# Which of the block-diagonal q rows go by VectorE copy and which by transfer: two and two in each half, against one and three, then three and one

## The chip, the cores and the metric

The kernel runs on one core of one Trainium2 chip. The metric is the device time of one execution in microseconds (us), less is better. Before the change it was 1295.35 us (median of 5 runs, 1295.15 to 1295.88). Timed runs were of the fast state (within 1.5% of the fastest of the same kernel); the four single looks near the end are of unknown state, as a single run of one core always is.

## The reference, cut to what matters

Two layers, each an attention block and a token-mixing MLP, on 2048 tokens of width 1024. The change is in the attention block only. It has 32 heads of width 32, and each token sees eight tokens, its own and those 2, 4, ... 14 places back:

```python
off = jnp.arange(8) * 2
idx = pos[:, None] - off[None, :]
...
logits = jnp.einsum("bhsd,bhswd->bhsw", q, kg) * scale
attn = _softmax(jnp.where(mask, logits, -1e9), axis=-1)
o = jnp.einsum("bhsw,bhswd->bhsd", attn, vg)
```

## The kernel before

Even and odd tokens never meet, so a *unit* is one parity (1024 tokens) of one group of four heads (128 of the 1024 columns): 16 units a layer. Work on a unit is done in two *visits* of 512 tokens each; they are numbered 0 to 63 over both layers, and even ones begin a unit. In each visit TensorE does the scores of this unit, the values of the visit before, and two of the four query/key chunks of the **next** unit. Queries of both halves (n = 0, 1) are made in the first visit, keys in the second.

The scores of four heads are had from one matmul because q is laid out block-diagonally: `qB[u % 2]` has 128 partitions by four head blocks, and in head block h only partitions 32h to 32h+31 are not zero. So each half's q, which arrives as one 128x512 tile `qs`, has to be put into four places of 32 partitions each.

```python
    def qk_chunk(u, wts, part, n):
        ...                                     # eight matmuls into ps   (L352)
        ls = slice(n * 512, (n + 1) * 512)
        if part:
            nc.scalar.copy(out=kT[u % 2][:, ls], in_=ps[:])               # L356
        else:
            qs = gop.tile([P, 512], BF16, name="qs", tag="go")
            nc.scalar.copy(out=qs[:], in_=ps[:])                          # L359
            for h in range(HG):
                hp = slice(h * DH, (h + 1) * DH)
                if h < HG // 2 or u == 0:                                 # the changed line
                    nc.vector.tensor_copy(out=qB[u % 2][hp, h, ls], in_=qs[hp, :])            # L363
                else:
                    chain_("SP", lambda: nc.sync.dma_start(out=qB[u % 2][hp, h, ls], in_=qs[hp, :]))  # L365
        return mm

    def scores(u, b):
        ...
        for i in range(HB):                     # 4
            lo = (b * HB + i) * P
            for r in range(P // KG):            # 4: sixteen matmuls a visit
                ...
                mm = nc.tensor.matmul(dst, lhsT=k[:, lo + r * KG:lo + (r + 1) * KG],
                                      rhs=q[:, :, lo + r * KG:lo + r * KG + GW], start=True, stop=True)   # L383
        ...                                     # exponential on ScalarE (L386); mask on VectorE (L398)
```

GW is 40, 32 tokens and 8 more. So in the first visit of a unit only the sixteenth score matmul reads into the second half of q, by eight columns. The PSUM accumulator of the values is a pool of one; `norm` (L437, VectorE) has to read it before the next visit's values matmuls (L414, L418) may write it.

The softmax here doesn't subtract the row's maximum and nothing guards it: scores larger than these inputs give would overflow.

## Time and profile before

| | before |
|---|---|
| time, median of 5 | 1295.35 us |
| TensorE busy | 1276.5 of 1293.7 us |
| attention, first to last start of a query/key matmul | 139.96 + 139.34 = 279.30 us |
| one unit, median (scores of a visit to those of the second after it) | 8.86 us |
| copies into qB | 136, 282 ns each (median) |
| transfers into qB | 120, 1.8 us (median) from issue to landing, when all of the data has arrived |

The profile page of the kernel before: busy time by engine, then instruction packets in the queues, the chain of waits, and two groups of instructions (count, then busy us and mean ns of one, then idle time of the engine before them and what ended most of it).

```profile
PE 1276.5 (99%) x8286; PEld 593.7 (46%) x8442; DVE 417.3 (32%) x852; ACT 373.2 (29%) x628; POOL 2.4 (0%) x15
...
q8 instruction: 66, 1.08, 0.3%
...
PE 98%; issue 1%; DVE 0%; DMA 0%; ACT 0%; SPq 0%
...
L352 PE MATMUL m<-hT,wqk 128*128 128x512 bf16 x963 | 223.3, 379 | 6.2 <-issue 4.6
L363 DVE COPY qB<-qs 32x512 bf16<-32x512 bf16 x136 | 38.1, 280 | 90.5 <-ACT qs L359 89.2
```

TensorE is the bound; VectorE is busy a third of the time. A matmul's 379 ns is not its cost: in a stream one starts every 0.216 us. (The Trainium skill, "Perfetto Trace Analysis", warns at its head that matmul busy time is a bad metric because matmuls are pipelined; this trace agrees, 379 against 216 ns.) Hence lengths of stretches are used below, not busy time.

The view of stretches for the two attention stretches (columns: start:end, length, then busy time of PE, PEld, DVE, ACT, POOL with counts, clock, DMA share, GB/s):

```profile
66.43:206.39 139.96, 136.37 (x1735) 67.08 (x1763) 95.85 (x217) 91.01 (x152) 0.00 (x0) 1.00 0.19 55
706.54:845.88 139.34, 136.13 (x1733) 67.08 (x1763) 95.85 (x217) 90.91 (x152) 0.00 (x0) 1.00 0.20 56
```

Where TensorE waited for transfers shows in its list of waits over the attention of the first layer (total us, times, longest):

```profile
PE m L352 <- issue: 2.4, 15, 0.2
PE s L383 <- DMA qB<-qs: 0.4, 1, 0.4
```

And in the timeline of that unit (start, length, engine and line; in brackets the idle time before and what ended it):

```profile
156.39 2.87 SPq L365 DMA_DIRECT2D qB<-qs  x4
...
156.95 0.57 DVE L363 COPY qB<-qs 32x512 bf16<-32x512 bf16 x2
...
158.13 0.58 DVE L363 COPY qB<-qs 32x512 bf16<-32x512 bf16 x2 [0.60 <-ACT qs L359]
158.82 2.02 DVE L398 TENSOR_TENSOR Pm<-pc,band 32x640 bf16<-32x640 bf16 x4
160.88 0.69 DVE L437 TENSOR_TENSOR oT<-acc,rd 128x512 bf16<-128x512 f32 x1
...
161.81 0.46 PE L383 MATMUL s<-qB,kT 128*32 128x160 bf16 x15
...
162.63 0.23 PE L383 MATMUL s<-qB,kT 128*32 128x160 bf16 x1 [0.36 <-DMA qB<-qs]
```

Fifteen score matmuls start in time, and the sixteenth 0.81 us after the first, where 0.23 us is usual. It waited for the last of the four transfers. Normally that transfer, issued 3.14 us ahead of the scores, lands 1.3 us ahead of them; here it was issued at 158.67 and landed at 162.49, 3.8 us later. Three more units have this in a smaller size, too small for the list of waits: visits 18, 44 and 46, by 0.29, 0.07 and 0.20 us. With the 0.58 us of this one (visit 20), TensorE lost 1.14 us.

The DMA view of 160.3 to 161.5 us of the same trace (packets, MB, share):

```profile
DMA packets 3, 0.02 MB, mean 15 GB/s; under 512 B 0, under 2 KB 2, under 8 KB 2
...
q8 instruction: 1, 0.02, 4.6%
q1 hardware_dynamic: 2, 0.00, 1.3%
```

Only one packet is under way at first: a 16,384-byte packet of the instruction queue (a block of instructions being fetched) starts at 160.44 and takes 0.88 us, and only as it ends do two small packets of the transfer start. The packet records behind this view say more. The transfer is 32 packets of 1,024 bytes; 30 of them had started, and these two are the rest. A packet's record here does not name its DMA engine; that the two sat behind the fetch on one engine is read from this order.

### The profile page before, as it was taken

What the parts mean: (1) busy time and instruction counts of PE and PEld (TensorE: products, weight loads), DVE (VectorE), ACT (ScalarE), POOL (GpSimd) and SP (SyncE); (2) the same over time, 40 slices, a digit from 0 to 9 for tenths busy, and PEclk for the clock granted to TensorE, in tenths of its full rate; (3) what the DMA queues carried; (4) which work ended last, traced back from release to release, by engine and by line L of the source; (5) the groups of instructions that cost most, each with busy time, mean ns of one, the idle gap of its engine ahead of it and who ended that gap; (6) DMA issues with size and microseconds to landing.
All of it is one profiled execution on the core that took longest, in us unless ns stands there. A gap on an engine that the chain in (4) does not pass through costs nothing.

```text
span 1293.7 us, 19400 instructions
## 1 busy us (share of the span) xinstructions
PE 1276.5 (99%) x8286; PEld 593.7 (46%) x8442; DVE 417.3 (32%) x852; ACT 373.2 (29%) x628; POOL 2.4 (0%) x15
## 2 busy tenths in 40 slices
PE   9999999999999999999999999999999999999999
PEld 4444444444444444444444444444444444444444
DVE  7457767830000022322300667778100000111111
ACT  5456665541111100000023666644311111000000
POOL 0000000000000000000000000000000000000000
PEclk9999999999999999999999999999999999999999
DMA  7411123643222135456510111246422222334331
GB/s 236 82 44 48 51 80 122 204 138 90 65 78 80 57 101 148 124 155 147 130 33 1 46 51 49 80 151 209 125 66 86 78 59 78 105 106 135 118 92 33
DMA packets 201862, 125.54 MB, mean 97 GB/s; under 512 B 39984, under 2 KB 183600, under 8 KB 201776
## 3 DMA queue, kind: packets, MB, share of 16 engines
q1 hardware_dynamic: 201776, 124.30, 33.9%
q8 instruction: 66, 1.08, 0.3%
q14 instruction: 20, 0.16, 0.0%
HBM read 96.48 MB, written 16.78 MB: 88 GB/s over the span
## 4 chain that ended last, share of the span: by engine, by line
PE 98%; issue 1%; DVE 0%; DMA 0%; ACT 0%; SPq 0%
PE m L352 17%; PE s L594 15%; PE s L547 15%; PE m L467 8%; PE acc L547 7%; PE m L547 7%; PE acc L594 7%; PE m L594 7%; PE m L337 4%; PE m L255 4%; PE s L383 2%; PE acc L418 1%; PE acc L422 1%; PE m L268 0%; DMA qB<-qs 0%
## 5 line engine op out<-in xcount | busy, mean ns | idle before, releaser
L594 PEld LDWEIGHTS <-w 128*128 128x128 bf16 x1820 | 177.0, 98 | 210.2
L547 PEld LDWEIGHTS <-w 128*128 128x128 bf16 x1792 | 175.4, 98 | 211.4
L352 PE MATMUL m<-hT,wqk 128*128 128x512 bf16 x963 | 223.3, 379 | 6.2 <-issue 4.6
L547 PE MATMUL s<-h,w 128*128 128x512 bf16 x878 | 201.2, 379 | 0.8
L594 PE MATMUL s<-g,w 128*128 128x512 bf16 (+1 forms) x912 | 201.0, 374 | 0.7
L596 DVE SCALAR_TENSOR_TENSOR xo<-s,b_sb,xs 128x512 bf16<-128x512 f32 (+1 forms) x33 | 24.4, 739 | 532.9 <-PE s L594 527.6
L352 PEld LDWEIGHTS <-wqk 128*128 128x128 bf16 x1024 | 95.3, 98 | 117.9 <-issue 10.7
L398 DVE TENSOR_TENSOR Pm<-pc,band 32x640 bf16<-32x640 bf16 x256 | 123.5, 483 | 66.0 <-ACT pc L386 56.6
L467 PE MATMUL m<-wo,oT 128*128 128x512 bf16 x500 | 110.6, 379 | 0.8 <-issue 0.3
L547 PE MATMUL acc<-h,w 128*128 128x512 bf16 x440 | 103.1, 379 | 0.5
L594 PE MATMUL acc<-g,w 128*128 128x512 bf16 x436 | 99.7, 379 | 0.5
L547 PE MATMUL m<-h,w 128*128 128x512 bf16 x438 | 98.5, 379 | 0.5
L594 PE MATMUL m<-g,w 128*128 128x512 bf16 (+1 forms) x436 | 96.9, 376 | 0.6
L174 ACT ACTIVATE ln<-mv,eps 128x1 f32<-128x1 f32 x64 | 18.9, 295 | 221.1 <-DVE mv L182 184.9
L467 PEld LDWEIGHTS <-oT 128*128 128x128 bf16 x512 | 49.6, 98 | 60.3 <-issue 1.3
L554 ACT ACTIVATE g<-s,b_sb 128x1024 bf16<-128x1024 f32 x28 | 31.2, 1114 | 158.2 <-PE s L547 146.5
L363 DVE COPY qB<-qs 32x512 bf16<-32x512 bf16 x136 | 38.1, 280 | 90.5 <-ACT qs L359 89.2
L255 PE MATMUL m<-wv,hT 128*128 128x512 bf16 x250 | 55.6, 379 | 1.0 <-ACT hT L249 0.7
L337 PE MATMUL m<-wv,hT 128*128 128x512 bf16 x251 | 55.2, 379 | 0.3
L386 ACT ACTIVATE pc<-s,shift 128x640 bf16<-128x640 f32 x64 | 51.2, 800 | 12.2 <-PE s L383 12.1
L359 ACT CAST qs<-m 128x512 bf16<-128x512 f32 x64 | 37.5, 586 | 49.1 <-PE m L352 48.0
L356 ACT CAST kT<-m 128x512 bf16<-128x512 f32 x64 | 37.5, 586 | 46.4 <-PE m L352 46.4
(58 smaller groups left out, 675.1 us busy)
## 6 DMA issues: line engine op xcount, KB each, us to landing
w<-in_B_w_dram SPq DMA_DIRECT2D x56, 512.0 KB, 3.8
w<-in_B_w_dram SPq DMA_DIRECT2D x64, 448.0 KB, 4.5
wqk<-in_A_wqkv_dram SPq DMA_DIRECT2D x16, 512.0 KB, 4.8
xa<-xn SPq DMA_DIRECT2D x32, 256.0 KB, 2.2
xs<-xa SPq DMA_DIRECT2D x32, 256.0 KB, 3.1
wv<-in_A_wqkv_dram SPq DMA_DIRECT2D x8, 512.0 KB, 5.7
wo<-in_A_wo_dram SPq DMA_DIRECT2D x8, 512.0 KB, 6.0
xr<-in_A_x_dram SPq DMA_DIRECT2D x16, 256.0 KB, 3.3
```

Source lines behind the costliest of these rows:

```text
L255: r = nc.tensor.matmul(pss_[k, n][:], lhsT=hT[:, kt, cols(*order[k])], rhs=wv[n][kt // 4][:, kt % 4, :], start=(kt == 0), stop=(kt == KD - 1))
L337: nc.tensor.matmul(ps[:], lhsT=hT[:, kt, cols(c, i)], rhs=wv[n][kt // 4][:, kt % 4, :], start=(kt == 0), stop=(kt == KD - 1))
L352: mm = nc.tensor.matmul(ps[:], lhsT=wts[part][:, kt, (g % 2) * P:(g % 2 + 1) * P], rhs=hT[:, kt, lo:lo + 512], start=(kt == 0), stop=(kt = ...
L356: nc.scalar.copy(out=kT[u % 2][:, ls], in_=ps[:])
L359: nc.scalar.copy(out=qs[:], in_=ps[:])
L363: nc.vector.tensor_copy(out=qB[u % 2][hp, h, ls], in_=qs[hp, :])
L386: nc.scalar.activation(out=pc[:].rearrange("p (n t) h k -> p n (t h k)", n=2), in_=ss[:, :, 0:2 * HG * GW], func=ACT.Exp, scale=scale, bia ...
L398: mm = nc.vector.tensor_tensor(out=Pm[rp, :, s0:s0 + HB, r * KG:r * KG + GW].rearrange("p h t k -> p t h k"), in0=pc[rp], in1=mk, op=ALU.mult)
L467: mm = nc.tensor.matmul(ps[:], lhsT=oT[g][:, cols(c, i)], rhs=wo[n][g // 4][:, g % 4, :], start=(g == 0), stop=(g == NG - 1))
L547: nc.tensor.matmul(pairs[fl][0][dc], lhsT=wt[c][:, i, fl * P:(fl + 1) * P], rhs=h2[c][i][:, dc * 512:(dc + 1) * 512], start=(k == 0), stop ...
L554: nc.scalar.activation(out=g[fb][:, fl, :].rearrange("p (n d) -> p n d", n=2), in_=t[:], func=ACT.Gelu_apprx_tanh, bias=b1_sb[:, ft:ft + 1])
L594: nc.tensor.matmul(ap, lhsT=w2t[ft // HF][:, ft % HF, c::DIL], rhs=g[ft // GF][:, ft % GF, lo:lo + w], start=(ft == 0), stop=(ft == FT - 1))
```

## The change

The intent is to have less outstanding on the way from the later half to the scores: of the four rows of the first half, which have more time, three go by transfer; of the second half only one. Per unit there are four copies and four transfers before and after.

```diff
-                if h < HG // 2 or u == 0:
+                if h < 1 + 2 * n or u == 0:
```

## The prediction

> **What bounds the kernel.** TensorE. The page gives PE 99% busy, and the chain of waits ends 98% on PE. The changed line runs only in the two attention stretches, 66 to 207 us and 707 to 847 us; by the view of stretches they hold 137.4 of 141.0 and 136.8 of 140.0 us of PE work. VectorE is busy for 96 us of each 141, so it has room, and DMA engines for 20%.
>
> **What the change moves.** Per unit (8.85 us in the timeline) there are four copies and four transfers before and after: 136 copies and 120 transfers stay (group lines). A copy costs 282 ns on VectorE, an issue 0.51 to 0.59 us on SyncE, a transfer 1.8 us from issue to landing (source view). One copy moves from the first half to the second, one transfer the other way.
>
> **Critical path.** Times below are relative to the first score matmul of the next unit (timeline). Before: the transfers go out at -5.42, -4.86 (first half), -3.69, -3.14 (second). Normally they land at -3.6, -3.0, -1.9, -1.3, so nothing waits. The sixteenth score matmul alone reads the second half (eight columns of overlap), at +0.23. In four of 30 units the very last transfer lands late, at +0.39, +0.68, +0.16 and +0.29, and the sixteenth matmul starts at +0.52, +0.81, +0.30, +0.43 in place of +0.23: 0.29+0.58+0.07+0.20 = 1.1 us lost. (The waits name only the largest, 0.4 us.)
> I believe the lateness comes from instruction fetch sharing a DMA engine: the Trainium skill, "Runtime: NRT & Kernel Launch", section "Instruction fetch mechanics", says that instruction memory is refilled by DMA in 16 KiB blocks. The trace agrees: 66 packets of 1.08 MB on the instruction queue, each about 0.9 to 1.2 us long, some 9 to 10 us apart in attention; one starts at 160.44 us, and the transfer issued at 158.67 lands at 162.49.
>
> After: first half at about -5.42, -4.86, -4.27; second half once, at about -3.67. The last issue is 0.5 us earlier. With the worst landing seen outside a weight load (3.8 us) it arrives at +0.15, in time for +0.23; the third of the first half arrives at -0.5 at worst. So nearly all of the 1.1 us should go. The units beside the output-weight load (landings up to 5.0 us) keep 0.1 to 0.7 us.
>
> On VectorE the second half's third copy ends at about 105.55 in the unit whose mask began at 105.38, so masks and the normalisation after them move 0.17 us later. The normalisation must free the one accumulator before the next values matmul; the smallest margin there is 0.52 us, leaving about 0.35.
>
> **Prediction: 1294.5 us, range 1293.7 to 1295.9.** Faster by over 2%: 0.3%. Within 2%: 99.4%. Slower: 0.3%.
>
> **What would show it.** Copies and transfers unchanged in number and duration; three issues then one per unit; last landing near -1.8; score matmuls no longer waiting for a transfer; normalisation to values margin about 0.35 us; every other stage the same length to 0.2 us.
>
> **What would make it wrong.** (a) The built order on VectorE puts a copy behind the masks: the third copy is then 2 to 3 us later and scores may wait, some 0.3 us a unit, up to 9 us. (b) The 0.35 us margin is not enough once semaphore delay is counted: up to 0.2 us in 30 visits, 5 us. (c) Fetch blocks fall differently against the transfers, so that the first half's third one or the lone one is late: within 1 us. (d) Run-to-run spread, 0.7 us before, hides a gain this small.

## The result

The changed kernel took 1293.86 us (median of 5, 1293.71 to 1294.23), beside 1295.35 us for the kernel before: ratio 0.999, 95% interval 0.9976 to 1.0004. A ratio here is the mean time of one kernel's fast runs over the mean of the other's of the same rounds, so not quite the ratio of the medians. The timing alone cannot even exclude zero. The traces can.

The page after the change: the busy line and the same groups.

```profile
PE 1275.1 (99%) x8286; PEld 593.4 (46%) x8442; DVE 417.1 (32%) x852; ACT 372.8 (29%) x628; POOL 2.4 (0%) x15
...
q8 instruction: 66, 1.08, 0.4%
...
L352 PE MATMUL m<-hT,wqk 128*128 128x512 bf16 x963 | 223.3, 379 | 6.2 <-issue 4.6
L363 DVE COPY qB<-qs 32x512 bf16<-32x512 bf16 x136 | 38.1, 280 | 99.2 <-ACT qs L359 97.1
```

Copies are as many and as long as before. The view of the two attention stretches after the change:

```profile
65.62:204.71 139.09, 135.92 (x1735) 66.99 (x1763) 95.64 (x217) 90.81 (x152) 0.00 (x0) 1.00 0.20 57
704.86:843.94 139.08, 135.87 (x1734) 66.95 (x1763) 95.62 (x217) 90.81 (x152) 0.00 (x0) 1.00 0.20 56
```

Both layers now take the same time: 278.16 us from unrounded starts, 1.14 us less than before. TensorE's waits over the same window (66 to 207 us) no longer name a transfer; the second line is already of the stage after attention:

```profile
PE m L352 <- issue: 2.4, 15, 0.2
PE m L467 <- issue: 0.2, 1, 0.2
```

The timeline of visit 20 after the change:

```profile
155.29 2.42 SPq L365 DMA_DIRECT2D qB<-qs  x4
...
155.95 0.27 DVE L363 COPY qB<-qs 32x512 bf16<-32x512 bf16 x1
...
157.03 0.88 DVE L363 COPY qB<-qs 32x512 bf16<-32x512 bf16 x3 [0.81 <-ACT qs L359]
157.94 2.02 DVE L398 TENSOR_TENSOR Pm<-pc,band 32x640 bf16<-32x640 bf16 x4
159.99 0.69 DVE L437 TENSOR_TENSOR oT<-acc,rd 128x512 bf16<-128x512 f32 x1
...
160.71 0.46 PE L383 MATMUL s<-qB,kT 128*32 128x160 bf16 x16
```

The four issues end 0.45 us sooner (2.42 in place of 2.87 us after the first), all sixteen score matmuls go together, and the normalisation ends at 160.68, 0.03 us before the scores; before, it ended 0.24 us ahead of them.

The spans of the two traces differ by 1.94 us, more than attention gives. The other 0.81 us lies in the start-up, which the change does not touch: the first query/key matmul starts at 66.43 us before and 65.62 after. Everything else in the program, taken together, is 947.98 us in both.

### The profile page after: what moved, and what is told of

It reads as the page before. It is cut to its first block, busy times and chain, and to the rows that moved or that the text cites. A ratio compares the mean times of both kernels' runs of the same rounds, so it can differ in the third digit from the quotient of the medians.

```text
span 1291.8 us, 19417 instructions
## 1 busy us (share of the span) xinstructions
PE 1275.1 (99%) x8286; PEld 593.4 (46%) x8442; DVE 417.1 (32%) x852; ACT 372.8 (29%) x628; POOL 2.4 (0%) x15
## 3 DMA queue, kind: packets, MB, share of 16 engines
q8 instruction: 66, 1.08, 0.4%
## 4 chain that ended last, share of the span: by engine, by line
PE 98%; issue 1%; DVE 0%; ACT 0%
PE m L352 17%; PE s L594 15%; PE s L547 15%; PE m L467 8%; PE acc L547 7%; PE m L547 7%; PE acc L594 7%; PE m L594 7%; PE m L337 4%; PE m L255 4%; PE s L383 2%; PE acc L418 1%; PE acc L422 1%; PE m L268 0%; PE s L244 0%
```

## The experiments

The theory: a transfer is late when its data still waits on a DMA engine as an instruction fetch occupies that engine. The fetch is one packet; a transfer that it alone holds lands about 1.0 to 1.3 us after the packet's end. In the kernel before, the last transfer's data is on its way until about 1.3 us ahead of the scores, so a fetch starting about 2.0 to 1.35 us ahead holds it and still lets it land too late. The change brings the lone last transfer 0.4 us forward, which should close that window: its packets, undisturbed, have all started 2.10 us ahead of the scores, where those of the last transfer before the change take until 1.65. The chief rivals: scatter between runs; a lighter VectorE in the first half; and luck, the fetches of the changed kernel having merely fallen elsewhere.

Measured values of all, the attention sum being first to last query/key matmul in both layers and "lateness" how much the sixteenth score matmuls came over 0.23 us after the first. "Before" is the median of the kernel before in the same rounds. The attention sum of a layer ends before the scores of its last unit, so the 0.33 us that visit 30 of before_shift lost are not in its sum.

| kernel | rows by copy, first + second half | time, median (before) us | ratio, 95% interval | attention sum us | lateness us (visits) |
|---|---|---|---|---|---|
| before | 2 + 2 | 1295.35 | | 279.30 | 1.14 (18, 20, 44, 46) |
| after | 1 + 3 | 1293.86 (1295.35) | 0.999, 0.9976 to 1.0004 | 278.16 | 0 |
| after_again | 1 + 3 | 1293.68 (1295.02) | 0.9985, 0.9972 to 0.9999 | 278.16 | 0 |
| second_only | 2 + 3 | 1293.88 (1295.02) | 0.9991, 0.9978 to 1.0003 | 278.16 | 0 |
| first_only | 1 + 2 | 1293.92 (1295.02) | 0.999, 0.9977 to 1.0002 | 278.46 | 0.11 (26) |
| reverse | 3 + 1 | 1295.42 (1295.02) | 1.0, 0.9988 to 1.0013 | 279.21 | 1.04 (18, 20, 26, 40, 42, 46) |
| before_shift | 2 + 2 | 1295.25 (1294.74) | 1.0005, 0.9991 to 1.0018 | 278.62 | 0.78 (28, 30) |
| after_shift | 1 + 3 | 1294.14 (1294.74) | 0.9997, 0.9983 to 1.001 | 278.16 | 0 |
| all_copies | 4 + 4 | 1297.11 (1294.74) | 1.0016, 1.0003 to 1.0028 | 280.67 | 0 |
| zero_four | 0 + 4 | 1295.15 (1294.74) | 1.0002, 0.9989 to 1.0016 | 279.63 | 0 |
| first_only_s4 | 1 + 2 | 1294.24 (1294.81), one run | | 278.68 | 0.11 (26) |
| first_only_s8 | 1 + 2 | 1293.34 (1294.81), one run | | 278.16 | 0 |
| after_s4 | 1 + 3 | 1293.43 (1294.81), one run | | 278.16 | 0 |
| after_s8 | 1 + 3 | 1293.46 (1294.81), one run | | 278.16 | 0 |

### The same kernel again

> The changed kernel once more. Theory (late last transfer): the two attention stretches, first to last start of the query/key matmuls, sum to 278.2 us (279.3 before), no score matmul starts late for a transfer; time 1.1 to 1.5 us below before. The start-up, 0.80 us shorter in the first trace of the changed kernel, has nothing to do with the change and should scatter by that much between runs. Rival (run-to-run scatter made the whole gain): difference within 0.5 us of zero in this round.

Measured: attention 278.16 us, to the hundredth as in the first trace; 1.34 us below before. The start-up took 65.92 us this time. In the eight traces with the unchanged start-up it lay between 65.46 and 66.43, and the trace of the kernel before happened to be the longest. So the attention length after the change repeats, and the start-up scatters by itself. The kernel before has one trace only: how far its 1.14 us would vary from run to run was not looked at, and in its shifted version below the lateness is 0.78 us.

### One half at a time, and the mirror

```diff
-                if h < HG // 2 or u == 0:
+                if h < 2 + n or u == 0:          # second_only
+                if h < 1 + n or u == 0:          # first_only
+                if h < 3 - 2 * n or u == 0:      # reverse
```

> First half stays at two copies and two transfers; second half gets three copies and one transfer. Theory: the whole gain is here, since the lone transfer takes the earlier slot, -3.69 us before the scores: attention sum 278.2 us, no late sixteenth score matmul, time like the changed kernel (1.1 to 1.5 us below before). Rival (the gain comes from the lighter first half, one copy fewer on VectorE): attention sum 279.3, no gain.

Measured: 278.16 us, no late unit. The second half alone gives the whole attention gain, as expected. Its visit 18 is also the cleanest look at the mechanism. The fetch starts 1.98 us ahead of the scores, as in visit 18 of the kernel before (2.00 us ahead). In the kernel before, two transfers of the second half go out and the second is held; these are the timelines, before:

```profile
148.98 1.14 SPq L365 DMA_DIRECT2D qB<-qs  x2
150.16 2.09 SPq L344 DMA_DIRECT2D wqk<-in_A_wqkv_dram  x2
...
152.67 0.75 PE L383 MATMUL s<-qB,kT 128*32 128x160 bf16 x16
...
153.16 0.09 PEld L383 LDWEIGHTS <-kT 128*32 128x32 bf16 x1 [0.24 <-issue]
```

and with the second half alone changed (the first line joins the last transfer of the first half with the lone one, which a narrower view shows alone in the last line):

```profile
146.84 1.68 SPq L365 DMA_DIRECT2D qB<-qs  x2
148.56 1.28 SPq L344 DMA_DIRECT2D wqk<-in_A_wqkv_dram  x2
151.70 0.46 PE L383 MATMUL s<-qB,kT 128*32 128x160 bf16 x16
...
148.01 0.51 SPq L365 DMA_DIRECT2D qB<-qs  x1
```

The lone transfer goes out 3.69 us ahead of the scores and lands 1.86 ahead, unheld. In the kernel before, the transfer in that same slot also landed in time, 1.87 ahead; it is the one behind it, 0.55 us later, that landed 0.39 us after the scores began.

> First half gets one copy and three transfers; second half stays at two and two. Theory: the last transfer goes out at about -2.95 us, 0.15 to 0.2 later than before, so late landings stay and grow a little: attention sum 279.3 to 280.5 us, time 0 to 1.2 us above before. Rival (lighter first half gains): attention sum near 278.2, time 1 us below before.

A miss. Attention took 278.46 us, nearer to the rival's figure than to mine, although its last transfer goes out 2.96 us ahead of the scores, later than before. What it lost (0.30 us) was lost around visit 26, where the transfers run into the load of the output weights and land up to 5.1 us after issue. No fetch fell between 2.0 and 1.35 us ahead of the scores in that trace: they started 2.9 us ahead or more, or at 1.22 and 1.10. Whether that was luck is taken up below.

> The mirror of the change: first half three copies and one transfer, second half one copy and three transfers, same totals. Theory: the last transfer goes out at about -2.55 us, lands at -0.7 when undisturbed and up to +1.3 when an instruction fetch is in its way; 6 to 12 of 30 units late, attention sum 281 to 285 us, time 2 to 6 us above before. Rival (only totals of copies and transfers count, or scatter): attention sum 279.3, same time as before.

Half a miss. Six units were late, more than the four of before, but by little, 1.04 us in sum, and the time did not move. The step that failed: I let the lateness grow with the time of issue. It does not; when a held transfer lands follows from the end of the fetch, and from how many wait behind it, however early or late it was issued. In visits 18, 20, 44 and 46 the fetches began 2.4 to 2.5 us ahead of the scores and held all three transfers of the second half; the last one landed 2.6 to 3.1 us after the fetch's start (1.6 to 1.7 us after its end, where one that is held alone takes 1.0 to 1.3), 0.1 to 0.6 us past the scores' start. In visits 40 and 42 it was not held itself, but its issue came only 1.7 and 1.5 us ahead, the issue before it having taken long.

### Moving the instruction fetch

If fetches are the cause, more instructions at the very start should move the block boundaries against the program, and with them the late units.

```diff
-        for _ in range(14):
-            chain_("PE", lambda: nc.tensor.matmul(wm[:], lhsT=warm[:, 0:P], rhs=warm[:], start=True, stop=True))
+        for w_ in [512] * 8 + [16] * 54:
+            chain_("PE", lambda: nc.tensor.matmul(wm[:, 0:w_], lhsT=warm[:, 0:P], rhs=warm[:, 0:w_], start=True, stop=True))
```

> The kernel before with 6 of its 14 warm-up matmuls replaced by 54 tiny ones: 96 more TensorE instructions ahead of everything (48 matmuls and their weight loads), nothing else. Theory (a late landing needs an instruction fetch that starts between about -2.0 and -1.35 us from the scores): the fetch comes about 20 instructions later in each unit than in the one before, so 96 instructions move the late units by about five units, from visits 18 and 20 to about 28 and 30, and from 44 and 46 to about 54 and 56; 18, 20, 44 and 46 are no longer late; sum of lateness of the order of 1 us, attention sum 278.5 to 280. Rival (the late units are fixed by the program's place, e.g. by the weight load that lies beside them): visits 18, 20, 44 and 46 are late again.

Measured: visits 28 and 30 were late, by 0.45 and 0.33 us; 18, 20, 44 and 46 were not. In the second layer the fetches came in visits 54 and 56 as expected (1.96 and 1.99 us ahead) and held the last transfers, but these landed 0.05 and 0.07 us after the scores' start, just before the sixteenth needs them. The timelines of visits 28 and 30, and the DMA view of 194.2 to 196.1 us, just ahead of visit 28:

```profile
196.19 0.46 PE L383 MATMUL s<-qB,kT 128*32 128x160 bf16 x15
196.88 0.23 PE L383 MATMUL s<-qB,kT 128*32 128x160 bf16 x1 [0.22 <-DMA qB<-qs]
...
205.52 0.79 PE L383 MATMUL s<-qB,kT 128*32 128x160 bf16 x16
```

```profile
DMA packets 49, 0.05 MB, mean 26 GB/s; under 512 B 16, under 2 KB 48, under 8 KB 48
...
q1 hardware_dynamic: 48, 0.03, 6.9%
q8 instruction: 1, 0.02, 4.8%
```

In visit 28 the wait for the transfer is named, and nothing but the fetch and that transfer is on the DMA queues: 30 of its 32 data packets had started 1.64 us ahead of the scores, the last two started as the fetch ended, 0.5 and 0.4 us ahead. In visit 30 it is 0.79 us from the first start to the last end, where 0.46 is normal. That is the strongest evidence for the fetch: 96 instructions in the start-up, with nothing changed in attention, move the late units of the first layer to the predicted ones.

> The changed kernel with the same 96 extra instructions. Theory (the lone last transfer has landed its data before the window in which a fetch can make it late): no late unit at all, attention sum 278.2. Rival (the changed kernel only happened to have its fetches at harmless moments): one to four late units, attention sum 278.5 to 279.5.

Measured: none late, 278.16 us. The same visit 30 is undisturbed; but its fetch came 0.33 us ahead of the scores here, not 1.91, so this visit alone does not test the change:

```profile
204.65 0.46 PE L383 MATMUL s<-qB,kT 128*32 128x160 bf16 x16
```

> The changed kernel with 4 more TensorE instructions. Theory: fetches that came at about -1.0 to -1.3 us come at about -1.4 to -1.7, after the lone transfer's data (landed at -1.7): no late unit, attention sum 278.2. Rival (luck): one or more late units.

> The changed kernel with 8 more TensorE instructions. Theory: fetches at about -1.9 to -2.1, the only place where the lone transfer can still be held at all; 2.05 us later is +0.15 against a need at +0.23, so no late unit or one of at most 0.3 us if a fetch is a long one; attention sum 278.2 to 278.5. Rival (luck): late units as in the kernel before, sum 279 or more.

These two add 2 and 4 tiny matmuls to the 14 warm-up ones. Measured: no late unit, 278.16 us in both. The foretold moments came only in part: after_s4 had fetches 1.97 and 1.48 us ahead, but after_s8 none between 2.53 and 1.24, so it did not test the moment that it was built for. With five traces of the changed kernel and one with the second half alone, the luck rival can be judged at equal fetch moments. In the kernel before and its shifted version, nine fetches started between 2.00 and 1.37 us ahead of the scores. In eight of them the last transfer was held and landed between 0.05 and 0.68 us past the scores' start; in one (visit 2 of the shifted version, 1.55 us ahead) it got through. In the other kernels, four started between 1.98 and 1.88 ahead (visits 18 and 44 of second_only, 16 of after, 18 of after_s4) and two more at 1.48 and 1.30 (20 of after_s4, 54 of after_shift), and the lone transfer landed unheld, 1.71 to 1.88 ahead, in all six. Between 2.00 and 1.86 us alone that is seven held of seven, against none of four. So at equal moments the gain is not luck. One gap stays: in none of these six traces did a fetch start between 2.52 and 1.98 us ahead. At 2.52 the lone transfer was held and landed 0.26 us ahead of the scores; whether a long fetch a little later would make it late is not shown. Nor is the edge of the window sharp: in visit 20 of the kernel before, the fetch's record starts 0.27 us after the held packets would normally have started.

> The kernel with only the first half changed, plus 4 TensorE instructions at the start (2 tiny matmuls and their weight loads). That kernel lost only 0.11 us before, and beside the output-weight load; its fetches came -1.1 and -1.22 us from the scores in visits 20 and 48, just after the last transfer's data (sent at -2.96, landed at -1.1) was through. Four instructions of a matmul stream are 0.43 us. Theory (its small loss was luck of the fetch moment): fetches move to about -1.5 and -1.65, and visits 20 and 48 (or a neighbour) are late by 0.2 to 0.7 us; attention sum 278.6 to 279.6 us. Rival (three transfers first are as good as the full change): no late unit away from the output-weight load, sum at most 278.4.

> The same with 8 instructions. Theory: fetches near -2.0 and -2.1, still behind the edge at which the last transfer (data through at -1.3) is held: late by 0 to 0.5 us in visits 20 and 48 or their neighbours; attention sum 278.3 to 279.4. Rival: no late unit away from the output-weight load.

Both missed. Visits 20 and 48 kept their fetches at about 1.1 and 1.3 us ahead although instructions were added, no fetch fell into the window, and the only loss was again around visit 26 (278.68 us, and 278.16 with 8). In all three looks at this kernel the fetches avoid the window. I cannot say whether that is chance or whether the order of transfers, or the semaphore waits that come with it (94 of them in TensorE's queue, against 66 before), set the moment of the fetch. This stays open: the second-half part of the change is shown to work by itself; the first-half part also ran without fetch losses, for a reason that is not shown, and it is the one that loses beside the output-weight load.

### Fewer or no transfers in the second half

> All four rows by copy in both halves, no transfer at all. Theory: no score matmul late; but VectorE's masks and normalisation in the second visit come 0.29 us later than in the changed kernel, whose smallest margin from normalisation to the next values matmul was 0.28 us: margin near 0, so small new waits of TensorE for VectorE, up to 0.1 us a unit; attention sum 278.2 to 281. Rival (transfers were the only cost): attention sum below 278.1 and no new wait.

```diff
-                if h < HG // 2 or u == 0:
+                if h < HG or u == 0:             # all_copies
+                if h < 4 * n or u == 0:          # zero_four
```

Measured: 280.67 us and no lateness of scores, as the theory had it. The timeline shows the new wait, though the list of waits does not name it:

```profile
103.39 2.38 DVE L363 COPY qB<-qs 32x512 bf16<-32x512 bf16 x8
...
105.80 2.03 DVE L398 TENSOR_TENSOR Pm<-pc,band 32x640 bf16<-32x640 bf16 x4
107.85 0.69 DVE L437 TENSOR_TENSOR oT<-acc,rd 128x512 bf16<-128x512 f32 x1
108.20 0.26 PEld L383 LDWEIGHTS <-kT 128*32 128x32 bf16 x16 [0.42 <-issue]
...
108.60 0.19 PE L414 MATMUL acc<-Pm,v 128*32 128x8 bf16 x4
```

Eight copies run back to back, the normalisation ends at 108.54, and the values start 0.06 us later, 0.40 us after the scores in place of 0.29. From normalisation to values the margin is 0.05 us in unit after unit: that is the hand-over itself, so TensorE waits each time, and a unit takes 8.95 us (median) in place of 8.85 in the changed kernel. The timed loss is 2.4 us against before; of it, attention accounts for 1.4 us between the two traces.

> First half no copy and four transfers, second half four copies and no transfer; totals as before. Theory: the last transfer goes out at about -3.6 us and belongs to the first half; no late sixteenth matmul, but the first score matmul now waits on it (lands at -1.7, or up to +0.3 behind a fetch, needed at 0), so a few late units of up to 0.3 us; VectorE margin near 0 as with all copies; attention sum 278.2 to 281. Rival (fewer transfers in the second half is all that counts): attention sum 278.2 or less.

Measured: 279.63 us, no late first or sixteenth score matmul; the expectation held in its VectorE half only. In six units fetches about 3.1 us ahead held the last two transfers, and these still landed by 0.57 us ahead of the scores; the latest landing anywhere in this trace was 0.23 us ahead. The margin on VectorE was again 0.05 us. So neither "fewer transfers late" nor "fewer transfers" is what counts by itself: four copies in the second half are one too many.

## Why the prediction was right

The time fell in the range (1293.86 in 1293.7 to 1295.9), and the cause foretold, a last transfer held by an instruction fetch, is the one found. That the time lies inside the range owes something to luck: it is near the lower end, and the second round of the same kernel, 1293.68, is just outside.

- *"in time ... So nearly all of the 1.1 us should go."* Right in outcome: attention became 1.14 us shorter, all of it, in every trace of the changed kernel, and with the second half alone. But a step on the way was wrong. The prediction let the worst landing come 3.8 us after the issue, at +0.15, and called that in time for +0.23; by its own pairs (landed +0.16, started +0.30) that would still have been late, by some 0.06 us. It is the step that failed openly in reverse: a held landing does not move with the issue. What the traces show instead is that the lone transfer's packets are through before a fetch in the old window can hold them, and that when an earlier fetch or the weight load did hold it, it landed 0.25 us ahead of the scores at the latest (five traces of the changed kernel).
- *"The units beside the output-weight load ... keep 0.1 to 0.7 us."* Wrong: no loss was left there; in visit 26 the lone transfer landed 0.49 us ahead of the scores in the first trace. The kernel before had lost nothing there either (landing at +0.06).
- *Lateness by instruction fetch.* A belief then; now supported by before_shift, which moved the late units to the foretold visits in the first layer (in the second the fetches came as foretold, but the landings were just in time), and by the packets that start as the fetch ends.
- *"second half once, at about -3.67"*, landing near -1.8: measured -3.54 and -1.7. The third transfer of the first half goes out at -4.23 (foretold -4.27).
- *Margin of the normalisation "about 0.35 us"*: measured 0.28 us at the least, 0.32 in most units. The term that was mis-sized is the delay of the mask: 0.17 foretold, 0.22 measured (in visit 20, from the first copy of the second half to the mask 0.69 before, 0.91 after). It was enough, and cost nothing, because the hand-over needs 0.05.
- *"every other stage the same length to 0.2 us"* failed in one place: the start-up was 0.81 us shorter in the first pair of traces. It scatters by 1 us over eight traces whose start-up has the same instructions, so it is not taken for an effect of the change.
- The size: 0.85 us was foretold (1295.35 to 1294.5), 1.49 and 1.34 us were measured between medians. The traces account for 1.14 by attention. The rest is about the size of the start-up's scatter; that it is scatter was not shown.
- Risk (a), a copy behind the masks, did not come: the changed kernel's copies stand before them. Risk (b) did not come, but one more copy in the second half brings it, as zero_four shows. Risk (c) was the right thing to fear, and shifts of 4, 8 and 96 instructions found no case of it, with the gap in the fetch moments named above.

## What to carry to other kernels

When a small transfer has to be there at a fixed time, don't reckon with its median landing: look for the few that land late, compare them with the instruction queue's packets, and leave room for one fetch ahead of the need. Moving work between a copy and a transfer is free only while both have slack; here the second half bears three copies and not four. A gain of 0.1% is better shown by the length of the stretch that it lies in, which repeated to 0.01 us, than by the whole time, which scattered by 1 us.

## What the Trainium skill lacked or had wrong

- "Runtime: NRT & Kernel Launch", section "Instruction fetch mechanics", gives blocks of 16 KiB and calls the cost of crossing one "mostly hidden". The size agrees (packets of 16,384 bytes, 66 in a run). No list of waits here puts a stall of TensorE down to instructions, but the fetch costs in another way, which the page does not say: it holds other transfers, by up to 2.0 us (3.8 in place of 1.8 us), 1.14 us of TensorE time in this kernel.
- "DMA: Bandwidth & Descriptors", section "Queues, rings and completion order", says that an engine drains a whole packet of one row before it turns to another. The trace agrees, as far as packets without an engine's name can: a fetch packet took 0.88 to 1.45 us in the held cases of the kernel before and its shifted version, and the held transfer landed 1.0 to 1.3 us after its end. The page gives no time for a packet of this size, nor the warning that small transfers in a hurry sit behind it.
- The same section puts refill on row 14. Here, if the trace's queue number is that row, most of the instruction fetch ran on queue 8: 66 packets and 1.08 MB there, against 20 packets and 0.16 MB on queue 14.
- "Runtime: NRT & Kernel Launch" says that the next block is fetched while the current one runs, and no page says at which instruction of the block a fetch starts. The moment moved by about five units with 96 instructions, as a fixed distance would have it, but not at all in some units with 4 or 8, and by up to 1.1 us between two traces of the same kernel (visit 16 of the changed one, 1.88 and 2.99 us ahead).
